# Routed experts behind an attention: the last values in a memory of their own, the first list's head gathered ahead of them, and the first six columns of later lists addressed as soon as counted

## The chip, the cores and the metric

The kernel runs on one core of one Trainium2 chip. A core has a matrix engine (PE, with its weight loads shown as PEld), a vector engine (DVE), a scalar engine (ACT), GpSimd (POOL) and SyncE (SP), which run side by side and wait for each other through semaphores. Every engine works through its own instructions in program order. DMA queues are fed by SP, ACT and POOL; POOL also issues the indirect DMAs, which gather or scatter rows by a list of row numbers. The metric is the device time of one execution in microseconds, as the median of the runs.

## The reference

An attention over channels gives `x` (20224 tokens of 256), and a mixture of 8 experts is applied to it. Tokens are given to experts greedily by the size of the logit, and each expert takes at most 2528.

```python
qn = q / (norm(q, axis=1) + 1e-6);  kn = k / (norm(k, axis=1) + 1e-6)   # B, N, C = 4, 5056, 256
a = softmax(kn.transpose(0, 2, 1) @ qn / tau)                            # 256 x 256 for each batch
x = (v @ a).reshape(20224, 256)
logits = x @ w_gate                                                      # 8 experts
for idx in argsort(-logits.flatten()):                                   # greedy, cap = N // E = 2528
    tok, e = idx // E, idx % E
    if assigned[tok] < 0 and counts[e] < cap:
        assigned[tok] = e; counts[e] += 1
for e in range(E):
    mask = assigned == e
    out[mask] = relu(x[mask] @ w1[e]) @ w2[e]                            # 256 -> 1024 -> 256
```

## The kernel before

The kernel has three parts, which overlap.

**Scores and values.** `scores` (lines 279 to 330) sums the products of k and q for one batch in PSUM, chunk by chunk (five chunks of 1024 tokens), and softmax follows on DVE. The values `x` are `v` times the 256 x 256 matrix, in pairs of tiles of 128 tokens: `x_tiles` (line 221) multiplies a pair into a PSUM tile `px`, ACT copies it to `xs` (line 230), and `store_x` (line 233) writes `xs` to the DRAM tensor `x_d` from ACT's queue. `v` chunks are loaded by `load_v` (line 212) into nine rotating tiles `vr`, or into the tiles `ua` and `ub`, which later hold expert weights (`HOMES`, line 66). The logits of most chunks are worked out separately (`logits`, line 412) so that routing can begin before all values are there. Thirteen chunks (`TODO`, line 67) are left for the time in which the first expert's tokens are being found.

**Routing.** For each expert, `route` (line 520) finds on DVE the threshold over which its tokens lie: eight search rounds, each of which compares on DVE (line 635), counts on PE (lines 600 and 613) and returns to DVE. With the mask of tokens, `compact` (line 785) makes the list of row numbers. It scans the mask, works out offsets with two matmuls (lines 797, 798), and for each of 20 column groups of 128 list positions it finds by a matmul (line 815) and a comparison with a sum (ACT, lines 833 and 878, or DVE, line 849) in which column of the token grid each position lies. Some twenty instructions on 128x20 numbers (lines 863 to 930) turn that into `src` (row in `x_d`, line 917) and `idx` (row in the output, line 930).

**Experts.** Each expert's tokens go in chunks of up to four column groups (`CUT`; the first expert 2, 4, 4, 4, 4, 2). `load_x` (line 1111) queues one indirect gather per column group from `x_d` into `xg`; `gather` (line 1126) issues the next of the queue on POOL. The rows are transposed, by PE (`turn`, line 1254, through one PSUM tile `pt`) or by DVE and a DMA (`stage`, line 1169), and split into a high part `xH` (ACT) and a low part `xL` (DVE). `layer1` (line 1293) runs 48 matmuls for a chunk and splits the result into `hH` and `hL`; `layer2` (line 1332) runs 24 matmuls per column group, ACT copies `py` to `y`, and POOL scatters `y` to the output by `idx`.

**What sets the order.** The program order of the engines is written by a planner in the kernel (`Order`, line 950). It keeps a modelled time for PE (`o.pe`) and DVE (`o.dve`). Each matmul of the main work advances it by `o.tick`, and whenever it gets on, `hook` (line 976) puts in instructions of the side streams (routing, list building) that the model holds ready: DVE work by priority (`COMPACT_PRIO`, `EARLY_PRIO`), ACT work and PE work when their inputs should be there. `o.until(key)` advances the model until a stream has come to a point; it emits nothing for PE itself. `want(key, fn)` runs something once a point is reached. `turn` for the next expert's first chunk is placed by `next_turn` (line 1422), when the list is done and `GATHER_LAT` has passed.

**Around the change.** After all value pairs of `TODO`, the kernel closes the pools of the value part, opens those of the expert part, queues the gathers of the first two chunks, and keeps PE busy with 24 matmuls that nothing uses (lines 1408 to 1412) until the first rows are there:

```python
for c in range(2):
    load_x(0, c)
    while queue:
        gather()
load_x(0, 2)
...
for i in range(START_TICKS):
    o.tick(200)
    PE.matmul(idle, ...)
turn(0, 0, 0)
turn(0, 0, 1)
```

The gather's source is the whole of `x_d`, so it comes behind every store. The second chunk's transposes (lines 1443, 1444) stand between layer 1 and layer 2 of the first chunk.

Of the kernel before, what the change touches and what calls it, by code (L numbers as in the profile page):

```python
# [21 lines left out]
E, F = 8, 1024  # L22
# [8 lines left out]
LASTC = CAP - (NCOL - 1) * 128  # L31
GW = C + E
RB = 3
NACT = 11
# [18 lines left out]
BUFS_V = 9  # L53
RING = 3
HALVES = {(1, 4): RING}
PAD_W = 8
PAD_H = 24
# [8 lines left out]
HOMES = {(1, 0): "ub", (1, 1): "ub", (3, 1): "ua", (3, 2): "ua", (3, 3): "ua", (3, 4): "ua"}  # L66
TODO = ((3, 1), (3, 2), (3, 3), (3, 4), (1, 2), (1, 3), (1, 4), (2, 0), (2, 1), (2, 2), (2, 3), (2, 4), (3, 0))
# [13 lines left out]
START_TICKS = 24  # L81
# [14 lines left out]
def attention_moe(ctx: ExitStack, tc: tile.TileContext, q, k, vt, tau, wg, w1t, w2t, tabs, out):  # L96
# [111 lines left out]
    a_f = [apool.tile([128, 2, GW], F32 if b else F32R, name=f"a{b}") for b in range(B - 1)]  # L208
    a_hi = apool.tile([128, 2, GW], F32R, name="a_last")
    vs = {}  # L210

    def load_v(b, c):
        home = HOMES.get((b, c))
        vr = big(home) if home else vp.tile([128, 2048], F32, name="vr", bufs=BUFS_V)
        nc.sync.dma_start(vr, vt[b, c])
        vs[b, c] = vr.rearrange("p (a t n) -> p a t n", a=2, t=T)

    def x_rows(width=C):
        return vp.tile([128, TH * GW], F32, name="xs", bufs=4)[:, 0:TH * width].rearrange("p (t c) -> p t c", t=TH)

    def x_tiles(b, c, t, xs, width, tick=None):
        n = 2 if width == C else 1
        px = ps_x.tile([128, 512], F32, name="px")
# [14 lines left out]
    with ExitStack() as sctx:  # L238
# [19 lines left out]
        def x_tiles_0(c, t, xs, width):  # L258
            n = 2 if width == C else 1
            px = ps_x.tile([128, 512], F32, name="px")  # L260
# [133 lines left out]
        def gates(b, ac, aT):  # L394
# [6 lines left out]
            if b == B - 1:  # L401
                a_f.append(apool.tile([128, 2, GW], F32, name="a_last"))
# [9 lines left out]
        def logits(s):  # L412
            lg = ps_x.tile([128, 512], F32, name="px")
# [106 lines left out]
    def route(p, R):  # L520
# [228 lines left out]
        yield ve(COLS, 0.5)  # L749
        r["sc"] = prefix(r["mask"], "a")  # L750
# [34 lines left out]
    def compact(p):  # L785
        r = routed[p]
        sc = r["sc"]
# [13 lines left out]
        V.tensor_copy(first, po[:, 0:1])  # L801
        yield ve(COLS, psum=True)
        V.tensor_tensor(E_[:, 0:COLS], po[:, 128:128 + COLS], sc, op=OP.add)
        G = rtile("G", (128, NCOL * 128), BF)
        yield ve(NCOL * 128, 4, ptr=1)
        V.tensor_scalar(G, rgrid, first, None, op0=OP.is_ge)
# [4 lines left out]
        ended = []  # L811

# [5 lines left out]
        def by_act():  # L818
            todo = list(range(0, NACT, RB))
            held = []  # L820
            while todo or held:
                while todo and len(held) < 2:
                    g0 = todo.pop(0)
                    n = min(RB, NACT - g0)
# [5 lines left out]
                for i in range(n):  # L830
# [3 lines left out]
                                 accum_out=sgn[:, g0 + i:g0 + i + 1])  # L834
                yield "A", 200
                S.activation(ext[:, g0:g0 + n], pi[:, 0:n * W].rearrange("p (i w) -> p i w", w=W)[:, :, COLS:W], AF.Copy)
            ended.append(1)

        def by_dve():
            num = rtile("num", (128, NCOL))  # L840
            for g0 in range(NACT, NCOL, RB):
                n = min(RB, NCOL - g0)
# [3 lines left out]
                for i in range(n):  # L846
# [3 lines left out]
                                    op1=OP.add, accum_out=num[:, g0 + i:g0 + i + 1])  # L850
                yield ve(2 * n, psum=True)
                V.tensor_copy(ext[:, g0:g0 + n], pi[:, 0:n * W].rearrange("p (i w) -> p i w", w=W)[:, :, COLS:W])
            yield ve(NCOL)
            V.tensor_copy(at[:, NACT:NCOL], num[:, NACT:NCOL])
            ended.append(1)

        if p == 0:
# [4 lines left out]
            yield ve(NCOL)  # L862
            V.tensor_scalar(at[:, 0:NACT], sgn[:, 0:NACT], 0.5, COLS / 2.0, op0=OP.mult, op1=OP.add)
# [20 lines left out]
        if p:  # L884
            yield ve(NCOL)
            V.tensor_scalar(at, sgn, 0.5, COLS / 2.0, op0=OP.mult, op1=OP.add)
        k1 = rtile("k1", (128, NCOL), I32)
        yield ve(NCOL)
        V.tensor_scalar(k1, at, 3, None, op0=OP.bitwise_and)
# [479 lines left out]
    with tc.manual_schedule():  # L1369
# [9 lines left out]
        for i, (b, c) in enumerate(TODO):  # L1379
            for t in range(0, T, 2):  # L1380
                if t % TH == 0:
                    xs = x_rows()
# [145 lines left out]
```

## Time and profile before

| | |
|---|---|
| median of 3 runs | 1281.18 us (1277.91 to 1281.96) |
| the profiled execution's own time | 1281.94 us |
| its span, first to last instruction | 1279.2 us |
| PE busy | 1253.7 us, 98% |
| DVE busy | 842.8 us, 66% |
| ACT busy | 551.0 us, 43% |
| POOL busy | 395.1 us, 31% |
| last value matmul ends | 322.25 us |
| first expert's layer 1 begins | 334.53 us |

The profile gives for each instruction its start from the beginning of the span, its duration, its engine and its line. In a timeline, what stands in square brackets behind an instruction is how long its engine had stood idle just before it and what ended that. In the windows, PE, DVE and so on have their busy time in a stretch (with the number of instructions), and PEclk is the clock that PE was granted, 1.00 being full speed. Where several semaphores are waited for, the profile names the one that came last, which need not be the one that mattered. Matmuls overlap, so that the start of the next is a better measure than the duration of one.

### The profile page before, as it was taken

The numbers are of one execution on the slowest core, as the hardware profiler recorded it, in microseconds if no ns is written. First come the engines' busy times: TensorE is split into PE (matmuls) and PEld (weight loads), VectorE is DVE, ScalarE is ACT, GpSimd is POOL, SyncE is SP. The second block draws the span as 40 slices with busy tenths as digits, with TensorE's granted clock in tenths as the row PEclk, the third lists the DMA queues.
The fourth block names the chain that finished last, engine by engine and source line by source line (L and its number), as shares of the span: only waits on it lengthen the run. The fifth ranks groups of instructions, "written<-read, shape, count | busy, mean of one in ns | idle before, by whom it ended". The sixth has DMA issues, their size and how long they took to land.

```text
span 1279.2 us, 23255 instructions
## 1 busy us (share of the span) xinstructions
PE 1253.7 (98%) x8827; PEld 1117.8 (87%) x8827; DVE 842.8 (66%) x2153; ACT 551.0 (43%) x1273; POOL 395.1 (31%) x662
## 2 busy tenths in 40 slices
PE   7999999999899999999999999999999999999998
PEld 6889877888788888998999898988988998898998
DVE  6788595889479678878866877877744334434421
ACT  5567642335234443524443553453455334334331
POOL 1000000000243363244424533453344344335322
PEclk9999999999899999999999999999999999999999
DMA  8998983344224124222422431433143235323310
GB/s 290 364 391 318 394 305 127 132 155 179 67 84 151 38 67 139 84 92 65 157 67 87 148 107 36 147 122 97 64 155 120 78 104 163 106 66 103 111 62 33
DMA packets 67119, 178.29 MB, mean 139 GB/s; under 512 B 10944, under 2 KB 33344, under 8 KB 62400
## 3 DMA queue, kind: packets, MB, share of 16 engines
q1 hardware_dynamic: 39808, 97.54, 21.5%
q0 software_dynamic: 17664, 58.22, 14.1%
q10 hardware_dynamic: 9536, 21.06, 4.2%
q8 instruction: 69, 1.13, 0.4%
q14 instruction: 42, 0.34, 0.1%
HBM read 117.53 MB, written 59.24 MB: 138 GB/s over the span
## 4 chain that ended last, share of the span: by engine, by line
PE 85%; issue 5%; DVE 5%; POOL 2%; DMA 2%; ACT 1%; POOLq 0%; SPq 0%; DVEq 0%; ACTq 0%
PE py L1350 31%; PE ph L1316 30%; PE s L305 8%; PE px L226 8%; PE pc L600 2%; PE px L269 2%; PE px L417 1%; POOL out_dram L1359 1%; DMA xg<-x_d,src 1%; DVE acc_q L315 1%; DVE acc_k L315 1%; DVE hL L1324 1%; PE pi L815 1%; DMA ua<-in_q_dram 1%; ACT hH L1319 0%
## 5 line engine op out<-in xcount | busy, mean ns | idle before, releaser
L1350 PE MATMUL py<-ua,hH 128*128 128x256 f32 (+1 forms) x2560 | 449.9, 279 | 0.0
L1316 PE MATMUL ph<-xH,ua 128*128 128x512 f32 (+3 forms) x1312 | 410.9, 388 | 3.9 <-DVE hL L1324 2.1
L1350 PEld LDWEIGHTS py<-ua,hH 128*128 128x128 f32 (+1 forms) x2560 | 388.5, 187 | 2.3
L1350 PE MATMUL py<-ua,hL 128*128 128x256 f32 (+1 forms) x1280 | 356.6, 279 | 0.0
L1324 DVE SCALAR_TENSOR_TENSOR hL<-ph,hH 128x512 fp32r<-128x512 f32 (+3 forms) x328 | 218.8, 668 | 160.1 <-ACT hH L1319 150.8
L1316 PEld LDWEIGHTS ph<-xH,ua 128*128 128x128 f32 x1312 | 244.6, 189 | 51.3 <-DVE hL L1324 4.4
L1319 ACT ACTIVATE hH<-ph 128x512 fp32r<-128x512 f32 (+3 forms) x328 | 190.8, 582 | 220.2 <-PE ph L1316 210.8
L1359 POOL DMA_INDIRECT out_dram<-y,idx x160 | 158.8, 993 | 319.9 <-ACT y L1357 281.0
L1316 PE MATMUL ph<-xL,ua 128*128 128x512 f32 (+3 forms) x656 | 254.6, 388 | 1.0 <-DVE xL L1278 0.6
L1350 PEld LDWEIGHTS py<-ua,hL 128*128 128x128 f32 (+1 forms) x1280 | 239.2, 187 | 0.0
L1118 POOL DMA_INDIRECT xg<-x_d,src x160 | 163.3, 1021 | 98.1 <-issue 45.6
L1357 ACT ACTIVATE y<-py 128x256 f32<-128x256 f32 (+1 forms) x160 | 61.4, 384 | 287.6 <-PE py L1350 247.6
L305 PE MATMUL s<-ua 128*128 128x256 f32 (+1 forms) x640 | 145.9, 387 | 6.9 <-DMA ua<-in_q_dram 6.9
L305 PEld LDWEIGHTS s<-ua 128*128 128x128 f32 (+1 forms) x640 | 122.4, 194 | 27.0 <-issue 6.4
L1316 PEld LDWEIGHTS ph<-xL,ua 128*128 128x128 f32 x656 | 124.1, 189 | 24.7 <-DVE xL L1278 2.0
L314 ACT ACTIVATE sq<-ua 128x1024 f32<-128x1024 f32 (+1 forms) x80 | 76.3, 970 | 50.4 <-DMA ua<-in_k_dram 19.3
L1204 DVE TENSOR_TENSOR xL<-xT,xH 128x512 fp32r<-128x512 f32 (+1 forms) x68 | 44.9, 678 | 64.4 <-ACT xH L1201 55.8
L1129 POOL COPY spacer<-hH 1x1 f32<-1x1 f32 x128 | 26.8, 209 | 160.8 <-ACT hH L1319 155.1
L230 ACT ACTIVATE xs<-px 128x512 f32<-128x512 f32 x60 | 35.8, 597 | 62.9 <-PE px L226 62.8
L226 PE MATMUL px<-a,vr 128*128 128x256 f32 x256 | 59.0, 384 | 0.0
L335 POOL TENSOR_SCALAR ny<-ny 128x4 f32<-128x4 f32 x4 | 2.0, 506 | 183.5 <-ACT ny L334 183.5
L226 PEld LDWEIGHTS px<-a,vr 128*128 128x128 f32 x256 | 47.1, 190 | 5.8
(298 smaller groups left out, 1358.1 us busy)
## 6 DMA issues: line engine op xcount, KB each, us to landing
x_d<-xs ACTq DMA_DIRECT2D x39, 512.0 KB
ua<-in_k_dram SPq DMA_DIRECT2D x35, 512.0 KB
ua<-in_q_dram SPq DMA_DIRECT2D x35, 512.0 KB
via<-xs SPq DMA_DIRECT2D x33, 512.0 KB
xT<-via SPq DMA_DIRECT2D x132, 128.0 KB
vr<-in_vt_dram SPq DMA_DIRECT2D x14, 1024.0 KB
ua<-in_vt_dram SPq DMA_DIRECT2D x4, 1024.0 KB
xg<-x_d,src POOLq DMA_INDIRECT x160
```

The costliest lines, as they stand in the source:

```text
L226: mm = PE.matmul(px[:, i * C:i * C + width], lhsT=vs[b, c][:, kb, t + i, :], rhs=a_f[b][:, kb, 0:width], start=(kb == 0), stop=(kb == 1))
L230: S.activation(xs[:, t % TH:t % TH + n, 0:width], px[:, 0:n * width].rearrange("p (t c) -> p t c", t=n), AF.Copy)
L305: newest[0] = PE.matmul(sb[:, ib * C:(ib + 1) * C], lhsT=kt[:np_, t, ib * 128:(ib + 1) * 128], rhs=qt[:np_, t, :], start=(first and t == 0 ...
L314: S.activation(sq[:n, t0:t1], t_[:n, t0:t1], AF.Square)
L1118: P.indirect_dma_start(out=xg[:n, i, :], out_offset=None, in_=x_d, in_offset=bass.IndirectOffsetOnAxis(ap=idx[:n, col:col + 1], axis=0))
L1204: V.tensor_tensor(xL[:, kb, 0:k * 128].rearrange("p (i t e) -> p i t e", i=k, t=4), rows, xH[:, kb, 0:k * 128].rearrange("p (i t e) -> p i ...
L1316: PE.matmul(ph[:, 0:nt], lhsT=l[:, w], rhs=x_[:, kb, 0:nt], start=(i == 0), stop=(i == 5))
L1319: S.activation(hH[:, fb, 0:nt], ph[:, 0:nt], AF.Relu)
L1324: V.scalar_tensor_tensor(hL[:, fb, 0:nt], ph[:, 0:nt], 0.0, hH[:, fb, 0:nt].bitcast(F32), op0=OP.max, op1=OP.subtract)
L1350: PE.matmul(py[:n, 0:C], lhsT=l[:, fb, tk], rhs=w[:, d], start=(j == 0), stop=(j == 23))
L1357: S.activation(y[:n], py[:n, 0:C], AF.Copy)
L1359: sd = P.indirect_dma_start(out=out, out_offset=bass.IndirectOffsetOnAxis(ap=idx[:n, col:col + 1], axis=0), in_=y[:n], in_offset=None)
```

## The change

It has four parts.

1. *A memory of their own for the last values.* The pools of the value part are split in two. The chunks (3,3) and (3,4) are loaded into two tiles of a pool (`vp_l`) that stays open longer, and with it the tiles `xs` and two of the four PSUM tiles `px`. The rotating tiles `vr` become seven instead of nine. `TODO` puts these two chunks last, `HOMES` and `LOADS` are arranged for it.
2. *The first expert's list in two parts.* `compact` first makes a list from the mask without its last 16 columns (those of the chunks (3,3) and (3,4)) and takes its first four column groups (`HEAD`). Then it takes these tokens out of the mask and makes the remaining 16 groups from the rest. The first four gathers read only `x_d[0:LATE_ROW]`, the rows ahead of the last two chunks.
3. *The head's gathers and transposes ahead of the last values.* The last six pairs (`LATE`) of values come after the pools of the expert part are open. Ahead of the last of them the four gathers of the head are issued and the first chunk is transposed whole (`turn_both`); the gathers of the second chunk's last two groups follow after the pairs. The 24 idle matmuls go. The second chunk's transposes move into layer 2 of the first chunk, the second half of them behind 12 matmuls of its second group.
4. *Later lists.* The address work of `compact` becomes a stream `addresses(a, b)`. For the experts after the first, the first six groups get theirs as soon as these are counted, the other 14 at the end; `done["first", p]` lets the first chunk's gather be queued then.

The core of the diff, with lines of plain renaming left out:

```diff
+LATE = 6
+LATE_ROW = (B * NCH - 2) * CH
+HEAD = 4
+NACT = {HEAD: 2, NCOL - HEAD: 9}
-BUFS_V = 9
+BUFS_V = 7
-         (3, 0): [(2, 2)], (3, 1): [(2, 3)], (3, 4): [(2, 4), (3, 0), (3, 1), (3, 2), (3, 3), (3, 4)]}
+         (3, 0): [(2, 2)], (3, 1): [(2, 3)], (3, 4): [(3, 3), (3, 4), (2, 4), (3, 0), (3, 1), (3, 2)]}
-HOMES = {(1, 0): "ub", (1, 1): "ub", (3, 1): "ua", (3, 2): "ua", (3, 3): "ua", (3, 4): "ua"}
+HOMES = {(1, 0): "ub", (1, 1): "ub", (2, 4): "ua", (3, 0): "ua", (3, 1): "ua", (3, 2): "ua", (3, 3): "late", (3, 4): "late"}
-START_TICKS = 24
...
+    lctx = ExitStack()
+    apool_l = lctx.enter_context(tc.tile_pool(name="apool_l", bufs=1, side="right"))
+    vp_l = lctx.enter_context(tc.tile_pool(name="vp_l", bufs=2, side="right"))
+    ps_xl = lctx.enter_context(tc.tile_pool(name="ps_xl", bufs=2, space=PSUM, side="right"))
-    ps_x = actx.enter_context(tc.tile_pool(name="ps_x", bufs=4, space=PSUM, side="right"))
+    ps_x = actx.enter_context(tc.tile_pool(name="ps_x", bufs=2, space=PSUM, side="right"))
...
     def compact(p):
+        mask = routed[p]["mask"]
+        if p > 0:
+            yield ve(COLS, 0.5)
+            sc = prefix(mask, "a")
+            yield from listed(p, sc, 0, NCOL)
+            return
+        head = rtile("mem")
+        yield ve(COLS)
+        V.tensor_copy(head, mask)
+        yield ve(16)
+        V.memset(head[:, COLS - 16:COLS], 0.0)
+        yield ve(COLS, 0.5)
+        sc = prefix(head, "a")
+        yield from listed(p, sc, 0, HEAD)
+        yield ve(COLS, 2, ptr=1)
+        V.tensor_scalar(sc, sc, routed[p]["first"], None, op0=OP.add)
+        yield ve(COLS)
+        V.scalar_tensor_tensor(head, sc, HEAD * 128.0, head, op0=OP.is_le, op1=OP.mult)
+        yield ve(COLS)
+        V.tensor_tensor(head, mask, head, op=OP.subtract)
+        yield ve(COLS, 0.5)
+        sc = prefix(head, "a")
+        yield from listed(p, sc, HEAD, NCOL)
...
+        def addresses(a, b):
+            cs_, n = slice(a, b), b - a
...
+            V.copy_predicated(src[:, cs_], early[:, cs_], w3_[:, cs_])
+            for col in range(a, b):
+                r["src", col] = src
+            if a == 0:
+                r["time"] = o.pe
+                done["first", p] = True
+            if b == NCOL:
+                while not done.get(("first", p)):
+                    yield "W", 0
+                done["idx", p] = True
...
+            if g == 0:
+                o.add(addresses(0, 2 * RB), lambda: COMPACT_PRIO).quick = True
+        yield from addresses(2 * RB if p else c0, c1)
...
         def fetch(i, col, n):
-            P.indirect_dma_start(out=xg[:n, i, :], out_offset=None, in_=x_d,
-                                 in_offset=bass.IndirectOffsetOnAxis(ap=idx[:n, col:col + 1], axis=0))
+            rows = x_d[0:LATE_ROW] if p == 0 and col < HEAD else x_d
+            P.indirect_dma_start(out=xg[:n, i, :], out_offset=None, in_=rows, in_offset=bass.IndirectOffsetOnAxis(
+                ap=routed[p]["src", col][:n, col:col + 1], axis=0))
...
+    def turn_both():
+        xg = xgs[0, 0]
+        ready[0, 0] = 2
+        nt = n_of(0, 0)
+        xH, xL = xts[0, 0] = (ffx.tile([128, 2, 512], F32R, name="xH"), ffx.tile([128, 2, 512], F32R, name="xL"))
+        pt = ps_t.tile([128, 512], F32, name="pt")
+        for i in range(cuts[0][0]):
+            for kb in range(2):
+                PE.transpose(pt[:, kb * nt + i * 128:kb * nt + (i + 1) * 128].bitcast(F32R),
+                             xg[:, i, kb * 128:(kb + 1) * 128].bitcast(F32R), identr)
+        for kb in range(2):
+            rows = pt[:, kb * nt:(kb + 1) * nt]
+            S.activation(xH[:, kb, 0:nt], rows, AF.Copy)
+            V.tensor_tensor(xL[:, kb, 0:nt], rows, xH[:, kb, 0:nt].bitcast(F32), op=OP.subtract)
...
-            want(("idx", p_), lambda: load_x(p_, c_))
+            want(("idx" if c_ else "first", p_), lambda: load_x(p_, c_))
...
-        hH = ffx.tile([128, 8, 512], F32R, name="hH")
-        hL = ffx.tile([128, 8, 512], F32R, name="hL")
+        home = (ffx, ffx2)[chunks.index((p, c)) % 2]
+        hH = home.tile([128, 8, 512], F32R, name="hH", bufs=1)
+        hL = home.tile([128, 8, 512], F32R, name="hL", bufs=1)
...
+        pairs = [(b, c, t) for b, c in TODO for t in range(0, T, 2)]
+        for at_ in pairs[:-LATE]:
+            pair(*at_)
         o.until(("ei", 0))
         settle()
         o.until(("idx", 0))
         actx.close()
         cctx.close()
...
         for c in range(2):
             load_x(0, c)
-            while queue:
-                gather()
+        head, queue[:] = list(queue), []
+        for n, at_ in enumerate(pairs[-LATE:]):
+            if n == LATE - 1:
+                queue[:] = head[:HEAD]
+                while queue:
+                    gather()
+                turn_both()
+            pair(*at_)
+        lctx.close()
+        ffx2 = ctx.enter_context(tc.tile_pool(name="ffx2", bufs=1))
+        ps_2 = ctx.enter_context(tc.tile_pool(name="ps_2", bufs=2, space=PSUM))
+        queue[:] = head[HEAD:]
+        while queue:
+            gather()
         load_x(0, 2)
+        load_ahead(0, 0)
...
-        idle = ps_1.tile([128, 512], F32, name="ph")
-        for i in range(START_TICKS):
-            o.tick(200)
-            PE.matmul(idle, lhsT=wt[0, 0][0][:, 0:128], rhs=wt[0, 0][0][:, 512:1024], start=(i == 0),
-                      stop=(i == START_TICKS - 1))
-        turn(0, 0, 0)
-        turn(0, 0, 1)
...
                 if p == 0 and c == 1:
-                    turn(p, 1, 0)
-                    turn(p, 1, 1)
-                    layer2(p, 0, h[0], {})
+                    layer2(p, 0, h[0], {1: [turn_at(1, 0)], (1, 12): [turn_at(1, 1)]})
```

More of the change, by code (lines that the diff above doesn't have):

```diff
@@ L206, in attention_moe, with next_px @@
     vp = actx.enter_context(tc.tile_pool(name="vp", bufs=2, side="right"))
-    ps_x = actx.enter_context(tc.tile_pool(name="ps_x", bufs=4, space=PSUM, side="right"))
-    a_f = [apool.tile([128, 2, GW], F32 if b else F32R, name=f"a{b}") for b in range(B - 1)]
-    a_hi = apool.tile([128, 2, GW], F32R, name="a_last")
+    ps_x = actx.enter_context(tc.tile_pool(name="ps_x", bufs=2, space=PSUM, side="right"))
+    a_f = [(apool_l if b == 2 else apool).tile([128, 2, GW], F32 if b else F32R, name=f"a{b}") for b in range(B - 1)]
+    a_hi = apool_l.tile([128, 2, GW], F32R, name="a_last")
     vs = {}
+    px_at = [0, True]
+    def next_px():
+        px_at[0] += 1
+        return (ps_x if px_at[0] % 2 and px_at[1] else ps_xl).tile([128, 512], F32, name="px")
     def load_v(b, c):
         home = HOMES.get((b, c))
-        vr = big(home) if home else vp.tile([128, 2048], F32, name="vr", bufs=BUFS_V)
+        if home == "late":
+            vr = vp_l.tile([128, 2048], F32, name=f"vr{c}", bufs=1)
+        else:
+            vr = big(home) if home else vp.tile([128, 2048], F32, name="vr", bufs=BUFS_V)
         nc.sync.dma_start(vr, vt[b, c])
@@ L401, in gates @@
             if b == B - 1:
-                a_f.append(apool.tile([128, 2, GW], F32, name="a_last"))
+                a_f.append(apool_l.tile([128, 2, GW], F32, name="a_last"))
             S.activation(a_f[b] if b else a_hi, ac, AF.Copy)
@@ L412, in logits @@
         def logits(s):
-            lg = ps_x.tile([128, 512], F32, name="px")
+            lg = next_px()
             for kb in range(2):
@@ L801, in compact @@
         V.tensor_copy(first, po[:, 0:1])
+        r["first"] = first
         yield ve(COLS, psum=True)
@@ L818, in by_act @@
         def by_act():
-            todo = list(range(0, NACT, RB))
+            todo = list(range(0, nact, RB))
             held = []
@@ L840, in by_dve @@
             num = rtile("num", (128, NCOL))
-            for g0 in range(NACT, NCOL, RB):
-                n = min(RB, NCOL - g0)
+            for g0 in range(nact, nc_, RB):
+                n = min(RB, nc_ - g0)
                 pi = ps_c.tile([128, 512], F32, name="pi")
@@ L855, in by_dve @@
+            yield ve(nc_)
+            V.tensor_copy(at[:, c0 + nact:c1], num[:, c0 + nact:c1])
             ended.append(1)
+        k1 = rtile("k1", (128, NCOL), I32)
+        k2 = rtile("k2", (128, NCOL), I32)
+        k3 = rtile("k3", (128, NCOL), I32)
+        w1_ = rtile("w1_", (128, NCOL))
+        k4 = rtile("k4", (128, NCOL), I32)
+        w2_ = rtile("w2_", (128, NCOL))
+        early = rtile("early", (128, NCOL), I32)
+        w3_ = rtile("w3_", (128, NCOL), I32)
+        bt = rtile("bt", (128, NCOL))
@@ L1431, in next_turn @@
                         o.tick(100)
-                if done.get(("idx", p + 1)) and o.pe >= routed[p + 1]["time"] + GATHER_LAT:
+                if done.get(("first", p + 1)) and o.pe >= routed[p + 1]["time"] + GATHER_LAT:
                     turn(p + 1, 0, turns.pop(0))
```

168 lines of the change are left out of this document (81 added, 87 removed).

## The prediction

> **What bounds the kernel now.** I read the page first, then the windows (busy time and granted clock by stretch), then the timelines of PE, ACT, POOL and DVE around the place where the values end and the experts begin.
>
> ```profile
> span 1279.2 us, 23255 instructions
> PE 1253.7 (98%) x8827; PEld 1117.8 (87%) x8827; DVE 842.8 (66%) x2153; ACT 551.0 (43%) x1273; POOL 395.1 (31%) x662
> ```
>
> PE is the bound: it stands still for 25.5 us of 1279.2. Only what takes waiting, or work without use, from PE can pay. The windows show where that is:
>
> ```profile
> core 0: us, PE busy (x) PEld busy (x) DVE busy (x) ACT busy (x) POOL busy (x), PEclk, DMA share, GB/s
> 281.00:303.30 22.30, 22.30 (x119) 19.16 (x118) 21.67 (x69) 14.85 (x45) 2.73 (x2) 1.00 0.62 236
> 330.00:334.50 4.50, 0.91 (x4) 0.58 (x5) 0.69 (x2) 0.38 (x1) 3.59 (x4) 0.69 0.34 98
> 334.50:338.40 3.90, 3.90 (x19) 3.73 (x19) 1.05 (x3) 1.15 (x3) 1.28 (x2) 0.50 0.29 88
> 344.50:350.80 6.30, 6.30 (x72) 6.26 (x70) 2.77 (x7) 0.98 (x2) 2.06 (x3) 1.00 0.15 44
> 460.00:1279.00 819.00, 809.67 (x5961) 733.84 (x5959) 497.75 (x1309) 336.60 (x860) 324.95 (x548) 1.00 0.31 100
> ```
>
> From 460 on PE is idle for 9.3 us in 819, in pieces of about 1 us. The one large hole is before 334.5, with a stretch at half clock (0.50) behind it. PE's timeline there:
>
> ```profile
> 319.88 2.37 PE L226 MATMUL px<-a_last,vr 128*128 128x256 f32 x10
> 322.94 1.66 PE L1411 MATMUL ph<-ua 128*128 128x512 f32 x6 [0.69 <-ACT xs L230]
> 324.44 0.76 PE L600 MATMUL pc<-oh,ge 128*128 128x64 bf16 x20
> 331.28 0.28 PE L1273 MATMUL pt<-identr,xg 128*128 128x128 f32 x1 [1.77 <-DMA xg<-x_d,src]
> 332.94 0.37 PE L1273 MATMUL pt<-identr,xg 128*128 128x128 f32 x1 [1.37 <-DMA xg<-x_d,src]
> 334.53 0.54 PE L1316 MATMUL ph<-xH,ua 128*128 128x256 f32 x1
> 339.18 0.28 PE L1316 MATMUL ph<-xL,ua 128*128 128x256 f32 x1
> 339.30 0.40 PE L1316 MATMUL ph<-xH,ua 128*128 128x256 f32 x2
> 344.17 0.53 PE L1273 MATMUL pt<-identr,xg 128*128 128x128 f32 x4 [1.41 <-DVE xL L1278]
> 344.54 0.47 PE L1350 MATMUL py<-ua,hH 128*128 128x256 f32 x2
> 350.80 0.39 PE L1316 MATMUL ph<-xH,ua 128*128 128x512 f32 x1
> ```
>
> The last value tile ends at 322.25, the first expert's layer 1 starts at 334.53. Between lie filler matmuls (L1411), one search round of the second expert, four transposes and waits for the gather. Why the gather is late stands in ACT's and POOL's timelines:
>
> ```profile
> 306.08 0.60 ACT L230 ACTIVATE xs<-px 128x512 f32<-128x512 f32 x1 [0.61 <-PE px L226]
> 306.70 0.33 ACTq L236 DMA_DIRECT2D x_d<-xs  x1
> 321.19 0.33 ACTq L236 DMA_DIRECT2D x_d<-xs  x1
> 322.91 0.33 ACTq L236 DMA_DIRECT2D x_d<-xs  x1
> ```
> ```profile
> 328.43 0.95 POOL L1118 DMA_INDIRECT xg<-x_d,src  x1 [43.63 <-DVE cur L663]
> 329.69 1.40 POOL L1118 DMA_INDIRECT xg<-x_d,src  x1 [0.30 <-issue]
> 331.39 0.95 POOL L1118 DMA_INDIRECT xg<-x_d,src  x1 [0.30 <-issue]
> ```
> ```profile
> 303.10 0.17 DVE L917 COPY_PREDICATED src<-early,w__2660 128x20 int32<-128x20 int32 x1
> ```
>
> The row numbers (src) are there at 303.27, but the gather reads all of x_d and so stands behind the last store: issued 322.91, first gather 328.43. That is 5.52 us. The second gather is issued 1.26 us later, and its rows reach PE 3.25 us after that (332.94).
>
> **Part by part. What goes.** (1) 322.25 to 334.53 is 12.28 us; the search round (0.76, with a small second matmul 0.8) and four transposes (0.5, as the four at 344.17) are needed anywhere, so 11.0 us go if the rows are there in time. (2) The half clock goes if PE doesn't wait: half of 3.9, 1.95 us. (3) The 1.41 us wait in front of 344.17 is the second half of the second chunk's transposes waiting for the only transpose bank; those now lie inside layer 2, half a column group (12 matmuls) apart. From 344.54 to 350.80 lie 48 such matmuls and a search round of 0.8, so 12 take about 1.4 us and cover most of the wait; with ACT's evacuation of y in front I leave 0.4. Together 11.0 + 1.95 + 1.0 = 13.95 us.
>
> **What decides whether (1) goes.** The head's gather reads only rows ahead of chunks (3,3) and (3,4), so it waits for the store after the ninth pair from the end. A row counts the pairs behind that one:
>
> ```profile
> 307.00:322.90 15.90, 4.78 (x8) 1.00 0.38 149
> ```
>
> These are the evacuations (L230) from 307.00 to 322.90, eight. The ninth from the end is at 306.08, its store at 306.70. With the full 5.52 us the first head gather starts at 312.2, the second at 313.5, and the second's rows are there at 316.7. The head's own row numbers come earlier: the list now ready at 303.27 tests 20 column groups, the head 4. PE reaches the transposes, now ahead of the last pair, at 322.25 less one pair. The last two stores each follow one pair and are 1.72 us apart, so 320.5. Margin 3.8 us: no wait. The last pair then covers the evacuation to xH and xL; I leave 0.3 us for its end.
>
> The four gathers run beside DVE's search:
>
> ```profile
> 329.48 0.78 DVE L635 TENSOR_TENSOR ge<-low,th 128x1200 bf16<-128x1200 int16 x1
> ```
>
> The gather at 329.69, beside this comparison, took 1.40, its neighbours 0.95. So each may take 0.45 more; the second chunk's last gather pays up to 0.9 in two, the head nothing, out of its margin. [...]
>
> **What is new on the path.** The second chunk's third and fourth gathers (columns 4 and 5) read all of x_d, and the last store now comes after the last pair. PE ends that pair at 322.75; evacuation and store as before (0.66 behind it): 323.4. First gather 5.52 later at the latest, 328.9; the fourth column's rows 4.5 later: 333.4. Needed when layer 1 (48 matmuls 0.12 apart at full clock: one has 0.28 at 339.18, two have 0.40 at 339.30; 5.8) and one column of layer 2 (24 matmuls, 2.7) are through: 322.75 + 0.3 + 5.8 + 2.7 = 331.5. Wait 0 to 1.9, or 2.8 beside DVE. The lower end holds if the store takes less than the last one did:
>
> ```profile
> 322.90:325.30 2.40, 2.36 (x27) 1.92 (x28) 0.48 (x3) 0.00 (x0) 0.00 (x0) 1.00 0.32 109
> 325.30:326.50 1.20, 1.20 (x7) 0.95 (x7) 0.72 (x3) 0.00 (x0) 0.00 (x0) 1.00 0.03 5
> ```
>
> Nearly all its bytes had moved by 325.3 (109 GB/s, then 5), so 3 us are possible; I take 1.1. Behind such a wait, does the clock drop? After 1.41 us it stayed at 1.00 (344.5 on), after the 3.6 us idle of 330 to 334.5 it was 0.50. A wait up to 2.8 lies between; nearer the first, so nothing, with 1.95 us as the far end. By the Trainium skill (TensorE: Matmul & The Clock Gate, Part 1) the clock halves only after an idle window of about 3.4 us; by it also nothing is added, and with the half clock the result would be about 1271.
>
> **Work added.** On PE a second pair of offset matmuls, 0.2 us. On DVE a second list build for the first expert:
>
> ```profile
> 280.94 0.49 DVE L515 TENSOR_TENSOR_SCAN sc_a<-ones_r,mk 128x160 f32<-128x160 f32 x1
> 281.53 0.29 DVE L794 TENSOR_SCALAR rem<-sc_a 128x160 bf16<-128x160 f32 x1
> 301.57 0.18 DVE L889 TENSOR_SCALAR k<-at 128x20 int32<-128x20 int32 x1
> 301.66 0.17 DVE L892 TENSOR_SCALAR k<-at 128x20 int32<-128x20 int32 x1
> ```
>
> Some eleven instructions of 0.1 to 0.5 and 16 narrow ones 0.09 apart: about 4 us, in a stretch where DVE is full (21.67 of 22.30). So the second expert's search comes 4 us later. PE does not wait for it there: it has value tiles. Each later list gains 17 narrow instructions, 1.5 to 3 us of DVE. What hides both is the lead of the second list:
>
> ```profile
> L917 DVE COPY_PREDICATED src<-early,w__4241 x1: 184/184/184, 430.2 to 430.2; 128x20 int32<-128x20 int32 x1
> L917 DVE COPY_PREDICATED src<-early,w__5808 x1: 185/185/185, 539.9 to 539.9; 128x20 int32<-128x20 int32 x1
> ```
> ```profile
> 409.91 0.38 PE L815 MATMUL pi<-E__97,G 128*128 128x162 bf16 x3
> 458.44 0.45 PE L1273 MATMUL pt<-identr,xg 128*128 128x128 f32 x4
> 587.22 0.45 PE L1273 MATMUL pt<-identr,xg 128*128 128x128 f32 x4
> ```
>
> Complete at 430.4, needed at 458.44: 28 us. With PE 12 to 13 us earlier and DVE 4 later, 11 remain; four gathers alone take 7 (three steps of 1.26, then 3.25), among scatters more. The first six columns make up for it: they are tested before the second batch at 409.91, so their addresses come some 18 us ahead of 430.4. I book nothing for that; an earlier gather could spare PE the eight transposes, up to 1 or 2 us, which stays in the range. Expert 2 has 47 us (539.9 to 587.22). The fewer value buffers cost nothing as I read the load order: each load's slot is free before its turn.
>
> **Sum.** 13.95 − 0.3 − 1.1 − 0.2 = 12.35 us. The profiled execution's own time is 1281.94, 0.76 above the median of 1281.18: 1281.94 − 12.35 = 1269.6, less 0.76: **1268.8 us**.
>
> **Rivals.** *The wait moves to columns 4 and 5.* The last store is the slow kind, gathers take 1.40, and the clock halves: 2.8 − 1.1 + 1.95 and some 0.5 at the next chunk: 1273. For it: the 5.52 us; against: the bytes' early end. *The head waits all the same*: if the gather also waits for stores of later rows issued ahead of it, the last of these comes after the fourth late pair, about 319.5. Gather 325, rows 329.5, so PE waits 9 us from 320.5 and the half clock stays, but columns 4 and 5 then come in time: 1268.8 + 9 + 1.95 − 1.1 = 1278.7, no change. For it: today's gather waits for every store. Against it: dependencies go by rows, as the store of 322.91 did not wait for the one of 321.19 to land (5.52 us). *Slower: the search becomes the pacemaker of expert 1.* If the early columns bring nothing and its list falls behind, PE waits at expert 1's first transposes. It costs from the point where the lead, 11 us, falls below the gathers' 7; to undo 12.4 and lose 3.8 on top it must lose 20 us, five times the 4 booked: 1285 to 1288. For it: DVE is full where the search begins. Against it: from 460 on DVE has 497.75 us of work in 819.
>
> **Numbers.** The forecast has 0.70, the moved wait 0.14, the head's wait 0.11, the pacemaker 0.05. About 0.3% (3.8 us) is what a measurement can tell from no change. Below 1277.4: 0.70 + 0.14 + a quarter of 0.11 = 0.87; same 0.08; slower 0.05. Range: down to 1264.5 (no wait at columns 4 and 5, 1.1; nothing left at (3), 0.4; expert 1 without transposes, 2; 0.8 for the spread of the runs, 1277.91 to 1281.96), up to 1277, which leaves out the unchanged and slower cases.
>
> **What would show it.** L1411 gone; first gather about 312 instead of 328.43; layer 1 at about 323 at full clock; second chunk's layer 1 at 337 to 338 instead of 350.80; a wait of at most 3 us for columns 4 and 5; second list's first six columns more than 10 us ahead of the rest. A first gather after 320, or a wait of several us at expert 1's first transposes, proves me wrong.

## The result, and the profile after

The changed kernel takes 1287.57 us (median of 7 runs, 1283.4 to 1289.53) where the kernel before takes 1281.18 (7 runs, 1277.36 to 1283.69). The ratio is 1.0053, with an interval of 1.0031 to 1.0074: 6 to 7 us slower, where 12.4 us less had been forecast. The profiled execution took 1288.27.

The page of the changed kernel, to be held against the one of before:

```profile
span 1286.4 us, 23360 instructions
PE 1262.3 (98%) x8789; PEld 1121.8 (87%) x8789; DVE 860.8 (67%) x2298; ACT 550.7 (43%) x1273; POOL 397.5 (31%) x662
```

PE is busy 8.6 us longer with 38 instructions fewer. So most of the loss isn't waiting. Where the prediction looked, things went nearly as it said. POOL's and PE's timelines after:

```profile
314.44 1.19 POOL L1177 DMA_INDIRECT xg<-x_d,src_h  x1 [28.90 <-DVE bt L951]
318.43 0.94 POOL L1177 DMA_INDIRECT xg<-x_d,src_h  x1 [0.30 <-issue]
330.32 0.94 POOL L1177 DMA_INDIRECT xg<-x_d,src  x1 [10.95 <-DMA x_d<-xs]
```
```profile
323.31 0.65 PE L1354 MATMUL pt<-identr,xg 128*128 128x128 f32 x4
325.22 0.65 PE L241 MATMUL px<-a_last,vr 128*128 128x256 f32 x2
325.52 0.47 PE L1393 MATMUL ph<-xH,ua 128*128 128x256 f32 x1
338.06 0.51 PE L1332 MATMUL pt<-identr,xg 128*128 128x128 f32 x4 [0.50 <-DVE xL L1337]
340.00 0.39 PE L1393 MATMUL ph<-xH,ua 128*128 128x512 f32 x1
451.14 0.39 PE L1393 MATMUL ph<-xH,ua 128*128 128x512 f32 x1
```

The last of the head's four gathers goes 12 us ahead of the first one that still waits for the last store. Layer 1 follows the last value pair at 325.52 instead of 334.53, the second chunk begins at 340.00 instead of 350.80, and expert 1's first chunk at 451.14. The last row of the same place before:

```profile
462.51 0.46 PE L1316 MATMUL ph<-xH,ua 128*128 128x512 f32 x1
```

So the change was 11.4 us ahead at expert 1. The windows from 460 on say that the lead isn't lost in waiting either:

```profile
460.00:1286.00 826.00, 815.98 (x5920) 736.31 (x5918) 510.14 (x1412) 333.47 (x855) 323.15 (x541) 1.00 0.30 99
```

PE is idle for 10.0 us of 826, where it had been 9.3 of 819. What is longer is the work. The chain of waits in the last two experts, where no routing is left, first before and then after (start, duration, engine, product, matmuls):

```profile
1078.84 10.92 PE py L1350 x96
1089.75 10.94 PE ph L1316 x48
1100.70 10.92 PE py L1350 x96
1187.95 10.92 PE py L1350 x96
```
```profile
1080.39 11.31 PE py L1426 x96
1091.70 11.18 PE ph L1393 x48
1102.88 11.31 PE py L1426 x96
1192.36 11.31 PE py L1426 x96
```

The same 96 matmuls of layer 2 take 0.39 us more, the same 48 of layer 1 take 0.24 more: 118 ns each for 114, 233 for 228. That is 0.63 us in every full chunk of these two experts, at full clock and with no wait. Between 1078 and 1188 alone the change falls back by 2.9 us (from +1.55 to +4.41).

One loss is a wait, 5.0 us at expert 1 while its first chunk runs and its second gets ready. The timelines of DVE, POOL, PE and ACT:

```profile
430.25 0.17 DVE L924 TENSOR_SCALAR k<-at 128x14 int32<-128x14 int32 x1
436.71 2.50 DVE L1156 TENSOR_TENSOR ua<-ub,ua 128x512 fp32r<-128x512 f32 x4 [2.91 <-ACT ua L1153]
439.12 0.17 DVE L926 TENSOR_TENSOR w__3952<-w__3952,k 128x14 f32<-128x14 f32 x1
439.69 0.18 DVE L936 COPY_PREDICATED src<-early,w__3956 128x14 int32<-128x14 int32 x1
```
```profile
443.99 0.98 POOL L1177 DMA_INDIRECT xg<-x_d,src  x1 [0.30 <-issue]
453.55 0.99 POOL L1177 DMA_INDIRECT xg<-x_d,src  x1 [0.31 <-issue]
```
```profile
456.39 0.28 PE L1332 MATMUL pt<-identr,xg 128*128 128x128 f32 x1 [1.48 <-issue]
463.76 0.50 PE L1393 MATMUL ph<-xH,ua 128*128 128x512 f32 x1 [1.22 <-issue]
468.04 0.50 PE L1393 MATMUL ph<-xH,ua 128*128 128x512 f32 x1 [2.33 <-DVE base L687]
```
```profile
462.38 0.60 ACT L1396 ACTIVATE hH<-ph 128x512 fp32r<-128x512 f32 x1 [1.61 <-PE ph L1393]
466.66 1.08 ACT L1396 ACTIVATE hH<-ph 128x512 fp32r<-128x512 f32 x2 [3.17 <-PE pt L1332]
```

The addresses of the other 14 columns are begun before 430.25, broken off for layer 1's hidden halves and the split of the next weights, and done at 439.87, 9.5 us later than the whole list before (430.4). The four gathers of the second chunk leave from 443.99 to 453.55, and PE waits in three pieces. Only the first, 1.48 us, stands ahead of that chunk's transposes. The other two stand ahead of the last two of the eight groups of six matmuls in the first chunk's own layer 1. With three PSUM tiles for `ph`, these need the tiles of the fourth and fifth groups, and ACT reads those only at 462.38 and 466.66, though PE had gone on to the next groups at about 459.5 and 461. So 3.5 of the 5.0 us hang on late hidden halves and not on the second chunk's gathers.

### The profile page after: what moved, and what is told of

Read it like the earlier page. It is cut to its first block, busy times and chain, and to the rows that moved or that the text cites. A ratio compares the mean times of both kernels' runs of the same rounds, so it can differ in the third digit from the quotient of the medians.

```text
span 1286.4 us, 23360 instructions
## 1 busy us (share of the span) xinstructions
PE 1262.3 (98%) x8789; PEld 1121.8 (87%) x8789; DVE 860.8 (67%) x2298; ACT 550.7 (43%) x1273; POOL 397.5 (31%) x662
## 4 chain that ended last, share of the span: by engine, by line
PE 87%; issue 5%; DMA 3%; DVE 2%; POOL 2%; ACT 1%; SPq 0%; another core or an unknown queue 0%; POOLq 0%; ACTq 0%; DVEq 0%
PE py L1426 32%; PE ph L1393 32%; PE s L320 9%; PE px L241 7%; PE pc L615 2%; DMA ua<-in_q_dram 1%; PE px L284 1%; POOL out_dram L1437 1%; PE px L432 1%; DMA x_d<-xs 1%; DMA ua<-in_k_dram 1%; PE pi L855 1%; DVE hL L1401 0%; PE pt L855 0%; PE pc L341 0%
## 5 line engine op out<-in xcount | busy, mean ns | idle before, releaser
L1426 PE MATMUL py<-ua,hH 128*128 128x256 f32 (+1 forms) x2560 | 460.4, 281 | 0.0
L1437 POOL DMA_INDIRECT out_dram<-y,idx x156 | 154.9, 993 | 322.7 <-ACT y L1435 287.1
L1236 DVE STREAM_TRANSPOSE xs<-xg 128x512 f32<-128x512 f32 (+1 forms) x72 | 48.7, 690 | 8.7 <-DMA xg<-x_d,src 8.5
L241 PE MATMUL px<-a,vr 128*128 128x256 f32 x224 | 51.6, 384 | 0.0
```

The source lines that it names most:

```text
L241: mm = PE.matmul(px[:, i * C:i * C + width], lhsT=vs[b, c][:, kb, t + i, :], rhs=a_f[b][:, kb, 0:width], start=(kb == 0), stop=(kb == 1))
L1236: V.transpose(xs[:, 0:k * 256].rearrange("p (q b i e) -> p b i q e", q=4, b=2, i=k)[:, half], xg[:, 0:k, half * 128:(half + 1) * 128])
L1426: PE.matmul(py[:n, 0:C], lhsT=l[:, fb, tk], rhs=w[:, d], start=(j == 0), stop=(j == 23))
L1437: sd = P.indirect_dma_start(out=out, out_offset=bass.IndirectOffsetOnAxis(ap=routed[p]["idx", col][:n, col:col + 1], axis=0), in_=y[:n], i ...
```

## The experiments

The kernel before took 1276.5 to 1281.2 us on the chips used, so runs are compared by their ratio to it on the same chip; 0.0010 is 1.3 us.

**Do the tiles' places set the spacing?** The change puts `PAD_X` (16 floats, line 1481) at the head of the experts' pool, and small tiles ahead of that pool. Together they move xg, xH, xL, hH, hL and y up by 128 bytes in every partition, while the weights stay. Counted in remainders of 256 bytes, xH lay 0 from w1 and hH 64 from w2; now they lie 128 and 192. The first two runs undo the shift in the one kernel and make it in the other.

e1:

```diff
-PAD_X = 16
+PAD_X = 48
```

> The changed kernel with one number altered: the pad at the head of the experts' pool is 48 floats and not 16, which moves every tile of that pool by 128 bytes and so puts xH, xL, hH, hL and y at the same remainders of 256 bytes as in the kernel before. Theory A (where the tiles lie sets the spacing of the layers' matmuls): layer 2's matmuls of experts 6 and 7 follow each other at 113 ns instead of 118, a layer 2 of 96 takes 10.92 us instead of 11.31 and a layer 1 of 48 takes 10.94 us instead of 11.19; the 13.2 us lost at the layers come back, and the stall of expert 1's second chunk (5.2 us) stays: 1274, between 1271 and 1278. Theory B (the spacing goes with something else: the hidden halves in two pools, the added vector work, or chance from run to run): spacing stays 118 ns or changes with no order, 1284 to 1290.

1271.07 us (1269.0 to 1272.32), ratio 0.9933 (0.9918 to 0.9949). The chain (its first row is from expert 5, still at the slow pace, and is taken up further on):

```profile
1001.38 11.31 PE py L1426 x96
1079.80 10.94 PE ph L1393 x48
1090.74 10.92 PE py L1426 x96
```

e2:

```diff
         ffx = ctx.enter_context(tc.tile_pool(name="ffx", bufs=2))
+        ffx.tile([128, 32], F32, name="pad_x", bufs=1)
```

> The kernel before with a pad of 32 floats at the head of the experts' pool, nothing else: xH, xL, hH, hL and y get the remainders of 256 bytes that they have in the changed kernel. Theory A (place of the tiles): the layers' matmuls go to 118 ns (layer 2) and 232 ns (layer 1) in experts 6 and 7, 13 us are lost at the layers, 1294, between 1288 and 1298. Theory B (two pools, added vector work): the kernel before has neither, so 1281 with its own scatter, 1277 to 1284, and 113 ns in experts 6 and 7.

1294.91 us, ratio 1.0118 (1.0102 to 1.0135).

```profile
1088.44 11.31 PE py L1350 x96
1099.75 11.16 PE ph L1316 x48
```

In the last two experts the pad alone turns the one pace into the other, both ways. From ratio 1.0053 to 0.9933 it is worth 0.0120, 15.4 us. The two pools of hidden halves and the added vector work are in e1 too and not in e2, so theory B falls.

Next, which tiles. e3 moves hH, hL and y alone in the kernel before (`PAD_H` 24 to 56):

> The kernel before with the pad ahead of hH, hL and y at 56 floats and not 24: only these three move by 128 bytes, xH and xL stay. Theory A, if each layer goes by its own left operand's place: layer 2 at 118 ns, layer 1 still at 227 ns, so 0.39 of the 0.63 us per chunk and 8 us of the 13: 1289, 1285 to 1293. Theory B: 1281, 1277 to 1284, with 113 and 227 ns in experts 6 and 7.

1283.45 us, ratio 1.0031 (1.0019 to 1.0044), in the range that theory B gave; layer 2 was not slow as a whole:

```profile
1076.90 10.88 PE py L1350 x96
1087.78 10.95 PE ph L1316 x48
1141.85 22.54 PE py L1350 x192
```

Three of an expert's five layer 2s run at 113 ns, the last two, which follow each other behind the narrower last chunk, at 117 (22.54 for 192). In the kernel before these 192 take 21.78. Theory A, as put, missed more than half of its 8 us. e6 moves the same tiles in the changed kernel (`PAD_H` 24 to 56), so that hH is back at 64 from w2:

> The changed kernel with the pad ahead of the hidden halves at 56 floats and not 24: hH, hL and y get the remainders of the kernel before (128 of 256), xH and xL keep those of the change (160). If each layer goes by the place of its own operands: layer 1 232 ns, layer 2 back at 113 ns, 8 of the 13 us come back, 1279, 1276 to 1282. If layer 2 takes over a phase that layer 1 leaves, so that xH's place decides for both: 232 and 118 ns, 1287, 1284 to 1290.

1276.12 us, ratio 0.9972 (0.9961 to 0.9983): layer 2 came back without layer 1.

```profile
1081.13 11.16 PE ph L1393 x48
1092.29 10.89 PE py L1426 x96
```

e7 moves w2 and everything above it (`PAD_W` 8 to 40):

> The changed kernel with the pad between the two weight halves at 40 floats and not 8, which moves w2 and all that lies above it by 128 bytes: xH, xL, hH, hL and y get the remainders of the kernel before, w1 keeps its own, w2 goes from 64 to 192. If the place of hH and hL alone counts (or that of xH): 227 and 113 ns, 1271, 1268 to 1274. If it is the distance between w2 and hH: layer 2 at 118 ns, layer 1 at 227, 1279, 1276 to 1283.

1279.54 us, ratio 1.0001 (0.9991 to 1.0011), as expected for the distance: layer 1 is back, layer 2 isn't, though hH lies at the remainder that it had before.

```profile
1074.42 11.30 PE py L1426 x96
1085.72 10.89 PE ph L1393 x48
```

e12 moves all weights and all that lies above them together:

```diff
+    ffw.tile([128, 32], F32, name="pad_v")
     for i in range(2):
         ffw.tile([128, 2048], F32, name=f"ua{i}")
```

> The changed kernel with a pad of 32 floats ahead of all weight tiles, which moves w1, w2 and everything above them by the same 128 bytes: xH, xL, hH, hL and y now stand at the very remainders of the kernel before (32 and 128 of 256), w1 and w2 do not, and every distance between them is as in the change (xH 128 from w1, hH 192 from w2). If the distance between the two operands counts: 232 and 118 ns as in the change, 1287.6, 1284 to 1290. If the moving operand's or the hidden halves' own place counts: 227 and 113 ns, 1271, 1268 to 1275.

1279.11 us, ratio 1.0022 (1.0011 to 1.0033), between the two expectations, but its layers are the change's:

```profile
1072.15 11.31 PE py L1427 x96
1083.46 11.18 PE ph L1394 x48
```

In e1, e7 and e12 all tiles of the experts' pool stand at the very same places, and only the weights below them (with what lies between) differ. So the place of one operand alone doesn't decide. The distance between the two fits both layers: e12, with the change's distances, runs at the change's paces to 0.01 us, though all these tiles stand 128 bytes further. It is not the only reading that is left. Wherever a layer is fast, its weights stand where they stood in the kernel before, so each operand could also need a place of its own; no run moves both operands of a fast pair together, which would tell. (e12 takes 4 us less than the change by the ratios; PE waits 1.5 us at expert 1's second chunk there in place of 5.0, see below.) Three more pads ask which distances are good:

> The changed kernel with the pad at the head of the experts' pool at 32 floats: all of its tiles 64 bytes further than in the change, 64 short of the kernel before (xH at 224 of 256, hH at 64). It asks whether 128 bytes are a step of their own. If the good places lie 256 bytes apart and this one is half way, the layers take something between: 1271 to 1288. If what counts is the remainder of 64 bytes, this run is as the change, 1287, 1284 to 1290, but then the run with 48 floats should have been so too.

> The changed kernel with the pad at the head of the experts' pool at 64 floats: 64 bytes beyond the run with 48. The distances of 256 bytes that count if the runs so far are read rightly: xH ahead of w1 by 64, hH ahead of w2 by 128 (measured: xH at 0 gives 227 ns, at 128 and 192 gives 232 and 233; hH at +64 gives 113, at -64 gives 118, at 0 gives 120). If layer 1 wants xH at w1's own remainder and layer 2 wants hH at +64 and nothing near, 232 and 118 ns and 1287, 1283 to 1293. If the good distances are a band that reaches to 64 and 128, 1271 or less.

> The changed kernel with that pad at 56 floats, 32 bytes beyond the run with 48: xH 32 bytes ahead of w1's remainder, hH 96 ahead of w2's. If a half step of 64 bytes already misses, or the remainder of 64 bytes counts besides, 1280 to 1300; if a band of 64 bytes or more is good, 1271 within 2.

e8 took 1293.31 us, more than either of its expectations; e9 1284.88 and e10 1286.05, each in the first of its two ranges. All of it in one table; distances in bytes of 256, durations from the chain between 1070 and 1125:

| run | xH from w1 | 48 of layer 1 | hH from w2 | 96 of layer 2 | ratio |
|---|---|---|---|---|---|
| before | 0 | 10.94 | 64 | 10.92 | 1 |
| change | 128 | 11.18 | 192 | 11.31 | 1.0053 |
| e1 | 0 | 10.94 | 64 | 10.92 | 0.9933 |
| e2 | 128 | 11.16 | 192 | 11.31 | 1.0118 |
| e3 | 0 | 10.95 | 192 | 10.88 | 1.0031 |
| e6 | 128 | 11.16 | 64 | 10.89 | 0.9972 |
| e7 | 0 | 10.89 | 192 | 11.30 | 1.0001 |
| e8 | 192 | 11.19 | 0 | 11.51 | 1.0100 |
| e9 | 64 | 11.00 | 128 | 11.39 | 1.0045 |
| e10 | 32 | 11.20 | 96 | 11.26 | 1.0060 |
| e12 | 128 | 11.18 | 192 | 11.31 | 1.0022 |

Of the distances tried, layer 1 is best at 0 and layer 2 at 64. There is no broad band: 32 bytes further both are slow (1.0060 with an interval of 1.0039 to 1.0081; e9 1.0028 to 1.0062, e8 1.0084 to 1.0115), though layer 1 is nearly back at 64. The 10.88 of e3 doesn't fit the other rows at 192.

**What happens at expert 1?** e4 takes the early addresses out of the change:

```diff
-            if g == 0:
-                o.add(addresses(0, 2 * RB), lambda: COMPACT_PRIO).quick = True
-        yield from addresses(2 * RB if p else c0, c1)
+        yield from addresses(c0, c1)
```

> The changed kernel without the early addresses: each later list's addresses are worked out in one piece at its end, as in the kernel before; the front of the change stays. Theory A says nothing changes at the layers (118 ns). At expert 1: if the early six columns only let the first chunk start early, which then waits for the second chunk's gathers, the first chunk starts some 6 us later and the second without the waits of 1.48, 1.22 and 2.33 us: 1287.6 plus 0 to 2, so 1286 to 1291. Rival: the early piece's 17 extra vector instructions hold the rest of the list back, and without it the second chunk's gathers come 3 us or more earlier than 443.99: 1283 to 1285.

1290.77 us, ratio 1.0085 (1.0065 to 1.0104), in the first range; the rival falls. PE now waits at the transposes of expert 1's first two chunks, for the gathers (us in all, times, longest):

```profile
PE pt L1330 <- DMA xg<-x_d,src: 4.8, 4, 1.9
```

e14 does the same with the pad of 48:

> The changed kernel with the pad of 48 floats and without the early addresses. At the change's own pad the run without them took 0.3% more than the change against the kernel before (ratios 1.0085 and 1.0053). If the early six are worth the same where the layers run at 227 and 113 ns, 1271 plus 4: 1275, 1272 to 1278. If their worth there came from the slower layers, 1271.

1278.25 us, ratio 0.9980 (0.9970 to 0.9990). Against e1 the early addresses are worth 0.0047, 6 us, more than the 4 expected (0.0032 at the change's own pad). Without them PE waits 4.9 us for gathers: the list is there at 432.5, 12 us ahead of the first transposes at 444.91, but the first chunk's four gathers leave among scatters from 435.15 to 444.23, and the last rows reach PE at 447.34.

e5 works columns 6 to 11 out early as well and lets the second chunk go on these (with the pad of 48; the core of the diff, `EARLY` is 12):

```diff
-            if g == 0:
-                o.add(addresses(0, 2 * RB), lambda: COMPACT_PRIO).quick = True
-        yield from addresses(2 * RB if p else c0, c1)
+            if g < EARLY:
+                o.add(addresses(g, g + 2 * RB), lambda: COMPACT_PRIO).quick = True
+        yield from addresses(EARLY if p else c0, c1)
...
-            want(("idx" if c_ else "first", p_), lambda: load_x(p_, c_))
+            want(("first" if c_ == 0 else "second" if c_ == 1 and p_ else "idx", p_), lambda: load_x(p_, c_))
```

> The changed kernel with the pad of 48 floats and a second early piece: columns 6 to 11 of every later list have their addresses worked out as soon as they are counted, as columns 0 to 5 do, and the second chunk of an expert is gathered once these are there. Theory C (the second chunk of expert 1 is late because the working of its addresses, begun at 429.7, is broken off at 430.3 for layer 1's hidden halves and the split of the next weights and goes on at 439.1): the gathers of that chunk come over 5 us earlier, its waits go, and of the 1271.1 us 3.6 go: 1267.5, 1265 to 1269. Rival (GpSimd's own queue or a free buffer holds these gathers): they come when they came, 1271, 1269 to 1273.

1272.07 us, ratio 0.9936 (0.9922 to 0.9949), the same as e1. The chunk's gathers did come over 10 us earlier (429.56 for 440.23 in e1), and PE's waiting in the two layers and the transposes from 425 to 480 fell from 4.7 us to 1.3, so theory C holds there; but the time was not kept. By its first hidden halves, e5 was 2.8 us ahead of e1 at expert 1's last chunk (535.89 and 538.68) and 0.4 ahead at expert 2's first (574.05 and 574.48). In between PE waits 1.4 us for the search, which e1 does not show; what took the rest is open:

```profile
429.56 1.01 POOL L1182 DMA_INDIRECT xg<-x_d,src  x1 [0.16 <-issue]
```
```profile
538.14 0.42 PE L616 MATMUL pc<-oh,ge 128*128 128x48 bf16 x10 [1.37 <-DVE ge L651]
```

e1 has late hidden halves as well: two of ACT's, with 1.1 and 0.9 us of PE's waiting behind them. The profile puts their lateness down to PE, but by the trace the sums that they read had ended at 455.7 and 458.4, and nothing else shows that ACT could wait for:

```profile
458.18 0.60 ACT L1396 ACTIVATE hH<-ph 128x512 fp32r<-128x512 f32 x1 [2.54 <-PE ph L1393]
462.48 0.60 ACT L1396 ACTIVATE hH<-ph 128x512 fp32r<-128x512 f32 x1 [2.24 <-PE pt L1332]
```

The gathers of three chunks leave POOL meanwhile, the last nine back to back (449.44 to 459.94). e13 holds back the gathers of expert 1's third and fourth chunks by one chunk each:

```diff
         ahead = chunks.index((p, c)) + 3
+        due = list(held_x)
+        held_x.clear()
         if ahead < len(chunks):
-            p_, c_ = chunks[ahead]
-            want(("idx" if c_ else "first", p_), lambda: load_x(p_, c_))
+            (held_x if chunks[ahead] in ((1, 2), (1, 3)) else due).append(chunks[ahead])
+        for p_, c_ in due:
+            want(("idx" if c_ else "first", p_), lambda p_=p_, c_=c_: load_x(p_, c_))
```

> The changed kernel with the pad of 48 floats; the gathers of expert 1's third and fourth chunks are held back by one chunk each, so that no longer twelve gathers leave GpSimd back to back while layer 1 of expert 1's first chunk runs. If ScalarE's idle stretches there (2.54 and 2.24 us ahead of hidden halves whose sums TensorE had long ended, with nothing shown that it waits for) come from that burst of gathers, they go, and of the 3.6 us lost at the second chunk some 2 to 3 come back: 1268.5, 1266 to 1271. If they have another cause, they stay and so does the time, 1271, 1269 to 1274.

1268.77 us (1268.52 to 1269.61), ratio 0.9913 (0.9897 to 0.9930). POOL pauses between the gathers of the third and the fourth chunk, and the two late halves are nearly gone:

```profile
454.57 0.94 POOL L1177 DMA_INDIRECT xg<-x_d,src  x1 [0.30 <-issue]
463.01 0.98 POOL L1177 DMA_INDIRECT xg<-x_d,src  x1 [0.60 <-issue]
```
```profile
456.68 0.60 ACT L1401 ACTIVATE hH<-ph 128x512 fp32r<-128x512 f32 x1 [1.05 <-PE ph L1398]
458.46 0.60 ACT L1401 ACTIVATE hH<-ph 128x512 fp32r<-128x512 f32 x1 [0.17 <-PE ph L1398]
```

That is what the theory of the burst expected. But e12, which is the change's own program with its tiles moved, has the same burst (its gathers run to 461.58, too) and no late half:

```profile
457.26 0.60 ACT L1397 ACTIVATE hH<-ph 128x512 fp32r<-128x512 f32 x1
458.66 0.60 ACT L1397 ACTIVATE hH<-ph 128x512 fp32r<-128x512 f32 x1 [0.28 <-PE ph L1394]
```

So the burst alone doesn't make them late. In the profiles PE waits 2.7 us from 425 to 480 in e13 and 5.1 in e1, but the intervals of the two ratios overlap, so that the 2.6 us between them are not sure. What ACT waits for stays open, also because e13 changes the order of much that follows. e13 has the lowest median here, 0.9% below the kernel before.

**Was the gain at the front what the prediction took it for?** e11 (with the pad of 48) puts the head's gathers and transposes behind the last pair and lets them read all of `x_d`:

```diff
-            rows = x_d[0:LATE_ROW] if p == 0 and col < HEAD else x_d
+            rows = x_d
...
+            pair(*at_)
             if n == LATE - 1:
                 queue[:] = head[:HEAD]
                 while queue:
                     gather()
                 turn_both()
-            pair(*at_)
```

> The changed kernel with the pad of 48 floats and the first list's head put back behind the last value tiles: its four columns are gathered from the whole memory of values once the last pair is stored, the early counting stays. If the front's gain of the change comes from the memory told apart (the prediction's step), the first gather goes from 314 to 328 or later, layer 1 starts 11 to 13 us later and begins at half clock: 1283, 1280 to 1286. If the gain at the front came from something else (the split list, the second gather queue order, the filler gone), it stays near 1271.

1282.83 us, ratio 1.0030 (1.0017 to 1.0042): 0.0097 or 12.4 us over e1. The first gather stands behind the last store again, and the clock falls:

```profile
327.38 0.95 POOL L1177 DMA_INDIRECT xg<-x_d,src_h  x1 [44.03 <-DMA x_d<-xs]
```
```profile
330.00:340.00 10.00, 8.51 (x44) 7.80 (x45) 4.10 (x12) 3.11 (x9) 3.67 (x4) 0.61 0.23 67
```

## Why the prediction was wrong

**The front was right.** *(1) and (2)*, 11.0 us of waiting and 1.95 of half clock, went: layer 1 starts 0.30 us behind the start of the pair's last two matmuls, with no wait (0.3 booked), at full clock, and undoing it alone costs 12.4 us. It came at 325.52 instead of 323.05, as all of the front lay some 2 us later in that execution; in e1 the first gather left at 312.41 (312.2 forecast) and layer 1 began at 323.49. *(3)*: 0.50 is left of the 1.41 us wait (0.4 left in the sum). *Columns 4 and 5*: their gather left at 330.32 (328.9 given as the latest), and PE began the second chunk 14.5 us behind the first (14 to 15 given). The moved wait was small, and the rival of the waiting head did not happen. ("Nearer the first" fits the 1.1 us that the prediction booked as a wait, not the 2.8 of which it was said: that lies nearer the 3.6, and those were several pieces of idling. Only 0.50 us of waiting came there.)

**The step that failed** is the sum itself: 1281.94 − 12.35 takes every other term as unchanged, above all "From 460 on PE is idle for 9.3 us in 819", after which only waiting was counted and the 810 us of work were carried over as they stood. That work became longer by 15.4 us (the change against e1), because the pools of the experts moved by 128 bytes against the weights, and the spacing of both layers' matmuls goes with that. It is most of the 19 us between forecast and result. The prediction took the tiles' moves to be about buffers ("The fewer value buffers cost nothing") and priced no place. Nothing in the profile of before shows this price, since all 41 chunks there have the same distances; but the rows of 48 and 96 matmuls could have been named as a term that must stay. Neither of the signs named for being wrong came.

**The lead of the second list** was a second miss. "28 us", with 11 left, was read at expert 1's first chunk only. The early six columns served that chunk: its gathers began at 412.65, 31 us ahead of the next chunk's. But the list's rest came 9.5 us later, not 4, since DVE's order puts a weight split into it, and the second chunk, needed right behind the first, had no lead: PE waited 1.5 us for its last rows, in the change as in e1 and e12. The other 3.5 us that it waited there hang on ACT's late halves; the prediction has no term for them, and their cause is open. "I book nothing" for the early addresses was wrong in the good direction: they are worth 6 us. The 11 us of lead were about right (12 in e14), but the gathers that were to take 7 took 15 from the list's end to the last rows, among scatters.

The 1287.57 us lie in the pacemaker rival's 1285 to 1288, and that is luck: PE did not wait at expert 1's first transposes, and the search did not set the pace.

With the pad of 48 and the gathers spread, e13 takes 1268.77 us, 0.0087 below the kernel before or 11.1 us; the sum had said 12.35. That it equals the forecast is in part chance: its terms differ by some us each way, and it still waits 1.6 us for the second chunk's rows.

The kernel before had spacing to lose only in part: in its trace the matmuls of layer 2 follow each other at 116 to 118 ns in some chunks of experts 1 to 5 as well (118 from 631 us on, 114 from 607), at the same distances. e1 has one of 11.31 too, at 1001.38, while in the change's chain no layer 2 of 96 from 1000 us on takes less. And e3 and e7 have the same distances but 10.88 and 11.30 (and 22.54 and 21.76 for the last two). So the place decides which pace is likely, with something more that these runs don't settle.

## What to carry to other kernels

When a change adds or moves a tile, compare start-to-start times of untouched matmuls before and after; a pad in front of a pool is a cheap run that tells the tiles' place from the rest of a change. Ask of every lead not only whether the first consumer is served but also the second, and what the planner puts between. A gain at the front is only a gain at the end if each later stage keeps its pace, so follow the lead in milestones from stage to stage.

## What the runs showed of the hardware

The spacing of back-to-back matmuls goes with the places of their operands in SBUF, and moves of 32 to 128 bytes change it: 10.88 to 11.51 us for the same 96 matmuls, 10.89 to 11.20 for the same 48, at a granted clock of 1.00. Between e1 and e7 w2 moved by 128 bytes under tiles that stayed where they were, and layer 2 went from 10.92 to 11.30. The distance of the two operands fits best, but it is not the whole (10.88 and 11.30 at one distance), and its rule is open. The Trainium skill (SBUF — State Buffer, the section "SBUF: two separate sides") says that among the engines only the port pair shared by DVE and GpSimd is contended, and that PE waits for nobody. That is about one engine against another; no run here shows a second engine in this, and what the runs vary is the place of PE's own two operands.

By the Trainium skill (TensorE: Matmul & The Clock Gate, the section "Wait — 56ns, not 53.3ns?") a warm matmul of 512 columns follows the one before by N / 2.4 GHz and about 2.5 ns, 215.7 ns. The best here was 10.89 / 48 = 227 ns, with a weight load of 128 columns in front of each, so at no distance tried is that floor reached.
